# Two transformer layers on one core: the first chunk's normalization moved ahead of a weight split, loads reordered, pools with dependencies by tile, one set of maxima moved behind the second score step

## The chip, the cores and the metric

One core of a Trainium2 chip runs the whole program. The metric is the device time of one execution in microseconds (us); the time given for a kernel is the median of several executions. An execution that goes through the hardware profiler leaves a trace, and the profile is a set of views of that trace.

## The reference

`x` has 2048 rows of 448 numbers. Two layers are applied, and both use the same weights. Each layer is attention and a feed-forward part, each on a normalized copy of `x` and added to it:

```python
def _A_ref(x, wq, wk, wv, wo):          # 16 heads of 28, one k and one v for all heads
    q = (x @ wq).reshape(B, S, H, Dh).transpose(0, 2, 1, 3)
    k = x @ wk
    v = x @ wv
    scores = jnp.einsum("bhqd,bkd->bhqk", q, k) * (Dh ** -0.5)
    p = _softmax(scores, axis=-1)
    o = jnp.einsum("bhqk,bkd->bhqd", p, v)
    return o.transpose(0, 2, 1, 3).reshape(B, S, H * Dh) @ wo

def _B_ref(x, w_gate, w_up, w_down):    # 448 -> 1792 -> 448
    return (_silu(x @ w_gate) * (x @ w_up)) @ w_down

x = x + _A_ref(_layernorm(x), wq, wk, wv, wo)
x = x + _B_ref(_layernorm(x), w_gate, w_up, w_down)
# the same two lines once more, with the same weights
```

## The kernel before

**Precision.** Every float32 operand of a matmul is split into a high and a low part, and a product is high·high + high·low + low·high. So for weights there are a raw tile (`wr`, and `wq` for the other half), a high tile `wh`, made by a cast on ACT, and a low tile `wl`, raw minus high. For activations they are `xh` and `xl`.

**Order.** The instructions of each engine run in the order in which the program records them. The waits between engines are semaphores that the framework places from the accesses to tiles. For a pool opened without `reuse_waits`, the first use of a region that an earlier pool has held waits for the earlier pool as a whole; with `reuse_waits="tile"`, it waits for the tiles that have held just those bytes. DMAs go through two queues, that of SP and that of ACT, and eight semaphores are handed out to them in turn, so a DMA can also wait for the one eight places before it.

**Stages.** The 2048 rows are four chunks of 512 (`NC`). A layer has three stages.

*Projection.* Each chunk is normalized (`norm_steps`: statistics on DVE, the scale `rstd` on POOL, `xn` on DVE), transposed by PE against an identity (`flip`, L246), split into `xh` and `xl`, and multiplied with the weights of q, k and v. There are 16 units (chunk c, column group m), the groups in the order `TURN` = 3, 2, 0, 1, and each has 11 matmuls (`product_T`, L272). ACT copies the result out (L497, L498), and SP stores it to DRAM: q to `qd` (L499), k to `kt` (L502). DVE and POOL place v in `vsb` (`vt`, L505). From DRAM k comes back as `keys` (L357, split on POOL) and q as `qstack` (L134, L135).

*Attention.* `scores` runs 256 steps: 16 pairs of chunk and head group, 16 blocks of 128 keys each. A step has twelve matmuls (L567): nine into `three` (three banks of PSUM, two such tiles in turn) and three into bank 7. ACT takes the exp of both (`pt1` from bank 7 at L573, `pt` from `three` at L574), and two steps later eight matmuls (`pv`, L604) add to bank 6. Bank 7 is a single one, so the next step's part for it waits until `pt1` has been taken. The score matmuls also add a bound on each row's maximum, with its sign turned, so that the exps stay in range. `maxima(c)` computes these bounds for a chunk: four matmuls (L398) into a bank, a transpose on DVE (L400), a reduction and a split, a second transpose, and a store (L411) into `rows` of DRAM; `rows(i)` (L391) loads them into `qstack`. The maxima of chunks 0 to 2 are computed inside units 6, 10 and 14 of the projection, those of the last chunk in `finish`, behind the last unit and ahead of the first step, in bank 6:

```python
            while self.seen < len(self.order):
                self.project()
            if not full:
                self.maxima(NC - 1, (6,))
```

*Feed-forward.* `rest` runs the matmuls of `by_rows` (L292) for all groups of the 1792 columns, with ACT, DVE and POOL adding the results to `xres` (L739 to L743). The projection of the second layer is threaded into the end of the first layer's feed-forward part.

**The head.** The program starts with four loads of chunk 0 of x on SP's queue (L890, tiles of 128 rows into `xres`). PE runs `IDLE` transposes of the identity, whose result nobody reads (L898). `load_wqkv` loads the projection weights in two halves: z = 1 (half of wq, and wk) on ACT's queue, z = 0 (the other half of wq, and wv) on SP's. Each matrix comes by two DMAs (`rows3`, L130 and L131): the first 384 rows in one, and the last 64 rows, read twice into the two halves of the partitions, in the other. Behind them ACT's queue gets chunk 1 of x (L887), and SP's later gets chunks 2 and 3. `part(z)` makes `wh` and `wl` of one half, the 224 columns of q first and then the 32 of k or v (L189 on ACT, L191 on DVE for z = 1, on POOL for z = 0). Then this order is recorded:

```python
    fs, got = norm_steps(0)
    for f in fs[:5]:      # statistics and scale
        f()
    parts[0]()            # the z = 1 half: wh, wl
    for f in fs[5:]:      # xn
        f()
```

After this come the transposes of chunk 0, `parts[1]` and the units.

**A second pass.** `forward` runs once; it is run again with `full=True`, in a slower and safer form, if one of the softmax sums is out of range. With these inputs the second pass does not run.

Of the kernel before, what the change touches and what calls it, by code (L numbers as in the profile page):

```python
# [23 lines left out]
NC = S // 512  # L24
# [5 lines left out]
LEAD = 4  # L30
LIMIT = 2.0**40
TURN = (3, 2, 0, 1)
IDLE = 50


@with_exitstack
# [18 lines left out]
def forward(  # L55
# [14 lines left out]
    nc = tc.nc  # L70
# [96 lines left out]
    def load_wqkv(pool, first):  # L167


        wh = pool.tile([P, 4, 512], F32R, name="wh")  # L170
        wl = pool.tile([P, 4, 512], F32R, name="wl")

        def load(z):
            if first and not z:
                r = halves("wq2").bitcast(F32).rearrange("p a (b n) -> p (a b) n", n=256)
            else:
                r = wpool.tile([P, 4, 2, P], F32, name="wr").rearrange("p k b n -> p k (b n)")
            nc.gpsimd.memset(r[:, :, 252:256], 0.0)
            eng = nc.scalar if first and z else nc.sync
            rows3(r[:, :, 0:224], wq[:, 224 * z : 224 * z + 224], eng)  # L180
            rows3(r[:, :, 224:252], wk if z else wv, eng)
            return r

        def part(z, r):
            hi, lo = (w[:, :, 256 * z : 256 * z + 256].rearrange("p k (b n) -> p k b n", b=2) for w in (wh, wl))
            for cols, n0, n1 in ((r[:, :, 0:224], 0, 112), (r[:, :, 224:256], 112, 128)):
                raw = cols.rearrange("p k (b n) -> p k b n", b=2)
                if first:
                    nc.scalar.copy(hi[:, :, :, n0:n1], raw)  # L189
                    eng = nc.vector if z else nc.gpsimd  # L190
                    eng.tensor_tensor(lo[:, :, :, n0:n1], raw, hi[:, :, :, n0:n1], ALU.subtract)  # L191
                else:
                    split(hi[:, :, :, n0:n1], lo[:, :, :, n0:n1], raw)

        if first:
            r1, r0 = load(1), load(0)
            return [lambda: part(1, r1), lambda: part(0, r0)], (wh, wl)
        for z in (1, 0):
            part(z, load(z))
        return [], (wh, wl)  # L200
# [102 lines left out]
    class Attention:  # L303
# [86 lines left out]
            dst = qts[i % 3][28:125:32, :, :].rearrange("j z (b w) -> j (z b) w", w=32)  # L390
            nc.sync.dma_start(dst.bitcast(F32), src)  # L391

        def maxima(self, c, cands=ALL):


            pm = bank(cands)[1]
            for n, g in enumerate(TURN):
                nc.tensor.matmul(pm, kd[0:112, g, :], self.hi[g], start=(n == 0), stop=(n == 3))  # L398
            side = pers.tile([P, 512], F32, name="sg")
            nc.vector.transpose(side, pm)  # L400
            ng = pers.tile([P, 64], F32, name="ng")
            nc.vector.tensor_reduce(ng, side.rearrange("p (n k) -> p n k", k=8), AX.X, ALU.max, negate=True)
            two = pers.tile([P, 4, 2, 16], F32R, name="two")
            hi, lo = two[:, :, 0, :], two[:, :, 1, :]
            ng = ng.rearrange("p (b j) -> p j b", j=4)
            nc.vector.tensor_copy(hi, ng)
            nc.vector.tensor_tensor(lo, ng, hi, ALU.subtract)
            flat = pers.tile([P, P], F32, name="flat")
            nc.vector.transpose(flat, two.rearrange("p j z b -> p (j z b)").bitcast(F32))
            self.rowsof[c] = dram.tile([P, P], F32, name=f"rows{self.layer}_{c}")  # L410
            nc.sync.dma_start(self.rowsof[c], flat)  # L411
# [100 lines left out]
        def finish(self):  # L512

            wide.append(ALL)
            if self.layer:
                nc.scalar.activation(warm, halfn[:, 0:1], AF.Exp)
                if not full:
                    self.fetch((3, 2))
                    self.fetch((0, 1))
            while self.seen < len(self.order):  # L520
                self.project()
            if not full:
                self.maxima(NC - 1, (6,))
            for n in sorted(self.when):
                for f in self.when[n]:
                    f()
            self.advance(len(self.steps), NM + KC * LEAD)
            wide.append(LOW)

        def scores(self, ff):  # L530
            next(switch)
            with tc.tile_pool(name=f"at{self.layer}", bufs=1) as wp:
                woh = wp.tile([P, NG, D], F32R, name="woh")
                wol = wp.tile([P, NG, D], F32R, name="wol")
                on, accs, pts = {}, {}, {}
# [115 lines left out]
                for n in range(last):  # L651
                    i, kt = divmod(n, NT)
                    if kt == 4 and 2 < i + 2 < len(GR):
                        self.stack(i + 2)
                    if kt == 7 and 2 < i + 2 < len(GR):
                        self.parts(i + 2)
                    if kt == 9 and 2 < i + 2 < len(GR) and not full:
                        self.rows(i + 2)
                    if i in (2, 3) and kt == 8:
                        load_wo(i - 2)  # L660
                    if n == NT and ff.nxt:
                        ff.nxt.below(nc.sync)
                    if kt == 8 and 10 < i <= 11 + FG:
                        ff.W[i - 11] = weights(i - 11)
                    step(n)
                    if not full:
                        between_steps(n)
                    if n > 1:
                        pv(n - 2)
                    if full:  # L670
                        between_steps(n)
                    if n in due:
                        due.pop(n)()
                    if i in (5, 13, 14) and kt > 5:
                        for f in {5: fs, 13: fs1, 14: ff.second[0][:5]}[i][kt - 6 : kt - 5]:
                            f()
# [19 lines left out]
    class FeedForward:  # L696
# [157 lines left out]
            nc.vector.tensor_reduce(whole, row[0:1, 0:P], AX.X, ALU.min)  # L854

        def rest(self, xb):
            self.stage = xb.enter_context(tc.tile_pool(name=f"stage{self.layer}", bufs=2))
            self.xbp = xb.enter_context(tc.tile_pool(name=f"xb{self.layer + 1}", bufs=3))
            xd = xb.enter_context(tc.tile_pool(name=f"xd{self.layer}", bufs=1))
            self.xd = [xd.tile([P, 512], F32R, name=f"xd{c}") for c in range(NC)]  # L860
            dma(self.xd[0][64:128, :], self.X[0][0][0:64, 3, :])
            self.X[0] = (*self.X[0][:2], self.xd[0])
# [8 lines left out]
            for gi, fs in enumerate(groups):  # L871
# [6 lines left out]
                        if gi or c:  # L878
                            self.unit(gi, c, n)
                if gi == len(groups) - 2 and self.nxt:  # L880
                    self.nxt.w = load_wqkv(xb.enter_context(tc.tile_pool(name="wqkv1", bufs=1)), None)[1]
            if self.nxt:
                self.nxt.project()
            self.flush()
# [1 line left out]
    def load_x(c, eng):  # L886
        eng.dma_start(xres[:, 4 * c : 4 * c + 4, :], xs[:, 4 * c : 4 * c + 4, :])  # L887

    for t in range(4):
        nc.sync.dma_start(xres[:, t, :], xs[:, t, :])  # L890
    xb = ExitStack()
    at = Attention(0)
    at.pool = xb.enter_context(tc.tile_pool(name="stage_", bufs=3))
# [4 lines left out]
        nc.tensor.transpose(idle[:, 0:P], ident, ident)  # L898
    parts, at.w = load_wqkv(xb.enter_context(tc.tile_pool(name="wqkv0", bufs=1)), True)
    nc.gpsimd.memset(halfn, -0.5)  # L900
    load_x(1, nc.scalar)
    nc.scalar.activation(warm, halfn[:, 0:1], AF.Exp)
    nc.gpsimd.memset(bottom, 0.0)
    nc.gpsimd.memset(bottom[0:1, :], 1.0)
    fs, got = norm_steps(0)
    for f in fs[:5]:
        f()
    parts[0]()
    for f in fs[5:]:
        f()  # L910
    at.norms[0] = got
    for c in (2, 3):
        load_x(c, nc.sync)
    at.below(nc.sync)
    at.X = {c: xtile(xpool if c == 0 else xbp) for c in range(NC)}
# [18 lines left out]
    for layer in range(2):  # L934
# [6 lines left out]
        at = ff.nxt  # L941
# [28 lines left out]
```

## Time and profile before

| | us |
|---|---|
| median of 3 executions | 2043.53 |
| lowest, highest | 2042.91, 2044.38 |
| the profiled execution: span, first to last instruction | 2041.5 |
| PE busy | 2018.5 (99%) |
| ACT busy | 1311.0 (64%) |
| POOL busy | 536.7 (26%) |
| DVE busy | 460.0 (23%) |
| exps of the 512 `three` tiles (L574) | 741.2 |
| mean granted PE clock over the span, full = 1 | 0.995 |

By the trace the first layer's projection ends at about 70 us, its attention runs from 72 to 596, and the feed-forward part to 1040; the second layer's projection ends at about 1079 and its attention at 1604.

The page and the views use one form of line: engine, line of the kernel, operation, destination <- sources, partitions x elements and type, count. In the timeline a line begins with the start and the time until the end of the group, and the bracket at its end names how long the engine had been idle and what released it. `PEld` is the load of the stationary operand into PE, `SPq` and `ACTq` are the DMA issues of the two queues. In the windows the columns are the stretch, its length, the busy time of PE, PEld, DVE, ACT and POOL in it with their instruction counts, the granted clock, the share of the 16 DMA engines and GB/s. The chain of waits goes back from the last instruction, at each step to what released it.

### The profile page before, as it was taken

Reading aid. Unit: us, or ns where it says so; the run is one execution under the profiler, and the core shown is the slowest. Engines: PE = TensorE matmul, PEld = TensorE weight load, DVE = VectorE, ACT = ScalarE, POOL = GpSimd, SP = SyncE. Lnnn points to the kernel's source line nnn. Section 1 sums busy time; section 2 is a strip of 40 time slices with the busy share of each in tenths; the row PEclk is TensorE's granted clock in tenths of the full one; section 3 lists DMA queues with packets and bytes.
Section 4 is the critical chain, followed back from the end, with each engine's and each line's share of the span. In section 5 each row is a group of like instructions: output and inputs, shape, how many; then the busy total and the mean of one; then the engine's idle time right before and its main releaser. Section 6 shows DMA issues by size and latency. Waiting matters only on the chain.

```text
span 2041.5 us, 43675 instructions
## 1 busy us (share of the span) xinstructions
PE 2018.5 (99%) x18627; PEld 1275.7 (62%) x18627; DVE 460.0 (23%) x890; ACT 1311.0 (64%) x2152; POOL 536.7 (26%) x601
## 2 busy tenths in 40 slices
PE   8999999999999999999999999999999999999998
PEld 7533434334348999999883334343343689988887
DVE  6300101001104323222451001010011242232322
ACT  3699898997973333333348998979979533333332
POOL 4313121021302333333341221111222122333320
PEclk9999999999999999999999999999999999999999
DMA  4201000011100111100031110100110000111102
GB/s 146 66 22 28 21 12 22 12 37 27 32 12 19 31 31 31 31 16 26 21 93 34 30 30 12 22 12 22 27 45 13 25 17 20 31 31 31 31 1 74
DMA packets 76512, 63.44 MB, mean 31 GB/s; under 512 B 22904, under 2 KB 63224, under 8 KB 76312
## 3 DMA queue, kind: packets, MB, share of 16 engines
q1 hardware_dynamic: 74580, 58.93, 10.4%
q8 instruction: 147, 2.41, 0.5%
q10 hardware_dynamic: 1732, 1.66, 0.3%
q14 instruction: 53, 0.43, 0.1%
HBM read 47.72 MB, written 12.32 MB: 29 GB/s over the span
## 4 chain that ended last, share of the span: by engine, by line
PE 50%; ACT 46%; DVE 1%; issue 1%; DMA 1%; POOL 0%; ACTq 0%; SPq 0%; DVEq 0%; POOLq 0%
PE bank L292 39%; ACT pt L574 31%; ACT pt L573 15%; PE bank L272 4%; PE three L551 2%; PE bank L551 2%; PE bank L246 1%; PE bank L604 1%; DMA wr<-in_A_wk_dram 1%; PE three L567 0%; DVE xl L253 0%; DMA kt<-stage 0%; DVE xn L229 0%; PE bank L398 0%; DVE vt L505 0%
## 5 line engine op out<-in xcount | busy, mean ns | idle before, releaser
L574 ACT ACTIVATE pt<-three 128x1536 f32<-128x1536 f32 x512 | 741.2, 1448 | 0.0
L604 PE MATMUL bank<-pt,vsb 128*32 128x512 f32 x4096 | 547.0, 606 | 0.5 <-ACT pt L574 0.5
L567 PEld LDWEIGHTS three<-qstack,keys 32*128 32x128 f32 x4608 | 252.9, 183 | 449.7 <-ACT pt L573 393.2
L567 PE MATMUL three<-qstack,keys 32*128 32x512 f32 x4608 | 498.5, 426 | 2.3 <-DVE vt L505 1.1
L567 PE MATMUL bank<-qstack,keys 32*128 32x512 f32 x1536 | 493.5, 426 | 2.9 <-ACT pt L573 2.9
L292 PE MATMUL bank<-xh,wgh 64*128 64x512 f32 x1728 | 447.6, 390 | 0.4
L292 PE MATMUL bank<-xh,wgl 64*128 64x512 f32 x1404 | 368.2, 390 | 0.0
L573 ACT ACTIVATE pt<-bank 128x512 f32<-128x512 f32 x512 | 305.8, 597 | 74.3 <-PE bank L567 68.1
L292 PE MATMUL bank<-xl,wgh 64*128 64x512 f32 x1296 | 335.1, 390 | 0.0
L292 PE MATMUL bank<-wdh,h 64*128 64x448 f32 x1792 | 331.2, 364 | 1.2 <-ACT h L827 0.8
L292 PEld LDWEIGHTS bank<-xh,wgh 64*128 64x128 f32 x1728 | 262.9, 184 | 19.1 <-DVE xl L253 1.5
L743 POOL TENSOR_TENSOR xres<-stage,xres 128x448 f32<-128x448 f32 x108 | 127.4, 1199 | 497.9 <-ACT stage L742 497.9
L638 POOL TENSOR_TENSOR o<-o 128x512 f32<-128x512 f32 x32 | 41.1, 1285 | 821.5 <-DMA o<-rd 748.5
L292 PEld LDWEIGHTS bank<-wdh,h 64*128 64x128 f32 x1792 | 242.5, 184 | 15.2 <-issue 2.7
L567 PEld LDWEIGHTS bank<-qstack,keys 32*128 32x128 f32 x1536 | 244.3, 183 | 4.5 <-ACT pt L573 4.3
L299 ACT COPY seen<-bank 128x1 f32<-128x1 f32 x664 | 81.7, 163 | 247.3 <-PE bank L292 244.4
L292 PEld LDWEIGHTS bank<-xh,wgl 64*128 64x128 f32 x1404 | 216.6, 184 | 13.8
L292 PE MATMUL bank<-wdl,h 64*128 64x448 f32 x896 | 217.7, 366 | 0.0
L825 ACT ACTIVATE sg<-bank 128x512 f32<-128x512 f32 x112 | 67.3, 601 | 220.0 <-PE bank L292 214.9
L292 PEld LDWEIGHTS bank<-xl,wgh 64*128 64x128 f32 x1296 | 196.3, 184 | 10.5
L604 PEld LDWEIGHTS bank<-pt,vsb 128*32 128x32 f32 x4096 | 80.9, 108 | 190.0 <-issue 175.2
L826 DVE TENSOR_TENSOR sg<-bank,sg 128x512 f32<-128x512 f32 x112 | 77.4, 691 | 500.0 <-ACT sg L825 491.1
(115 smaller groups left out, 1736.6 us busy)
## 6 DMA issues: line engine op xcount, KB each, us to landing
o<-rd SPq DMA_DIRECT2D x32, 256.0 KB
qd<-stage SPq DMA_DIRECT2D x32, 224.0 KB
qraw<-qd SPq DMA_DIRECT2D x128, 56.0 KB
wdr<-in_B_w_down_dram SPq DMA_DIRECT2D x28, 224.0 KB
wr<-in_B_w_gate_dram SPq DMA_DIRECT2D x28, 192.0 KB
wr<-in_B_w_up_dram SPq DMA_DIRECT2D x28, 192.0 KB
out_dram<-xres SPq DMA_DIRECT2D x15, 224.0 KB
wrk<-kt SPq DMA_DIRECT2D x8, 256.0 KB
```

Source lines behind the costliest of these rows:

```text
L272: nc.tensor.matmul(po, a, b, start=(i == 0), stop=(i == len(seq) - 1))
L292: nc.tensor.matmul(po, a, b, start=start, stop=stop, skip_group_check=True)
L299: nc.scalar.copy(seen[:, i : i + 1], po[:, 0:1])
L551: nc.tensor.matmul(po[:, 0:D], a[:, g, ts_], b[:, g, :], start=(g + z == 0), stop=(g == NG - 1 and z == 2))
L567: nc.tensor.matmul(three[:, j, :] if j < 3 else one, k[js, kp, ks], q[js, part, :], start=(z == 0), stop=(z == 2), tile_position=(32 * j, 0),)
L573: nc.scalar.activation(pt1, one, AF.Exp, scale=SCALE)
L574: nc.scalar.activation(pt, three, AF.Exp, scale=SCALE)
L604: nc.tensor.matmul(accs[i][32 * j : 32 * j + 32, :], vsb[:, kt, :], pts[n][j], start=(kt == 0), stop=(kt == NT - 1), skip_group_check=True,)
L638: nc.gpsimd.tensor_tensor(rb, oraw, rb, ALU.mult)
L743: nc.gpsimd.tensor_tensor(r, s, r, ALU.add)
L825: nc.scalar.activation(sg, pg[0], AF.Silu)
L826: nc.vector.tensor_tensor(sg, pg[1], sg, ALU.mult)
```

## The change

- `IDLE` is 36 instead of 50.
- In `part`, POOL and DVE change places for the low parts: z = 1 on POOL, z = 0 on DVE.
- Of the four loads of chunk 0 of x, the second and fourth go to ACT's queue.
- Chunk 1 of x is loaded from SP's queue, together with chunks 2 and 3, and no longer from ACT's behind the weights.
- `xn` of chunk 0 is recorded ahead of `parts[0]`.
- The last chunk's maxima leave `finish`. They are recorded in `scores`, behind the second step, and still use bank 6.
- The pools `at`, `stage`, `xb`, `xd` of both layers and `wqkv1` of the second are opened with `reuse_waits="tile"`.

```diff
-IDLE = 50
+IDLE = 36
...
                 if first:
                     nc.scalar.copy(hi[:, :, :, n0:n1], raw)
-                    eng = nc.vector if z else nc.gpsimd
+                    eng = nc.gpsimd if z else nc.vector
                     eng.tensor_tensor(lo[:, :, :, n0:n1], raw, hi[:, :, :, n0:n1], ALU.subtract)
...
-        def maxima(self, c, cands=ALL):
+        def maxima(self, c, pm=None):
-            pm = bank(cands)[1]
+            pm = bank(ALL)[1] if pm is None else pm
...
             while self.seen < len(self.order):
                 self.project()
-            if not full:
-                self.maxima(NC - 1, (6,))
...
-            with tc.tile_pool(name=f"at{self.layer}", bufs=1) as wp:
+            with tc.tile_pool(name=f"at{self.layer}", bufs=1, reuse_waits="tile") as wp:
...
                     step(n)
                     if not full:
+                        if n == 1:
+                            self.maxima(NC - 1, banks[6])
                         between_steps(n)
...
-            self.stage = xb.enter_context(tc.tile_pool(name=f"stage{self.layer}", bufs=2))
-            self.xbp = xb.enter_context(tc.tile_pool(name=f"xb{self.layer + 1}", bufs=3))
-            xd = xb.enter_context(tc.tile_pool(name=f"xd{self.layer}", bufs=1))
+            self.stage = xb.enter_context(tc.tile_pool(name=f"stage{self.layer}", bufs=2, reuse_waits="tile"))
+            self.xbp = xb.enter_context(tc.tile_pool(name=f"xb{self.layer + 1}", bufs=3, reuse_waits="tile"))
+            xd = xb.enter_context(tc.tile_pool(name=f"xd{self.layer}", bufs=1, reuse_waits="tile"))
...
-                    self.nxt.w = load_wqkv(xb.enter_context(tc.tile_pool(name="wqkv1", bufs=1)), None)[1]
+                    self.nxt.w = load_wqkv(xb.enter_context(tc.tile_pool(name="wqkv1", bufs=1, reuse_waits="tile")), None)[1]
...
     for t in range(4):
-        nc.sync.dma_start(xres[:, t, :], xs[:, t, :])
+        (nc.scalar if t % 2 else nc.sync).dma_start(xres[:, t, :], xs[:, t, :])
...
-    load_x(1, nc.scalar)
...
     for f in fs[:5]:
         f()
-    parts[0]()
     for f in fs[5:]:
         f()
+    parts[0]()
     at.norms[0] = got
-    for c in (2, 3):
+    for c in (1, 2, 3):
         load_x(c, nc.sync)
```

## The prediction

> **What bounds the kernel now.** I read the page first: its span, the busy shares and the chain of waits that ended last.
>
> ```profile
> span 2041.5 us, 43675 instructions
> PE 2018.5 (99%) x18627; PEld 1275.7 (62%) x18627; DVE 460.0 (23%) x890; ACT 1311.0 (64%) x2152; POOL 536.7 (26%) x601
> PE 50%; ACT 46%; DVE 1%; issue 1%; DMA 1%; POOL 0%; ACTq 0%; SPq 0%; DVEq 0%; POOLq 0%
> 2.96 10.91 DMA wr<-in_A_wk_dram
> ```
>
> The chain alternates between the matmuls and the exps; the change alters neither their number nor their size. What it can move is the little that is neither: the head, where the fourth row (the chain in order of time) shows the wk load as the one long transfer, and the places where projection hands over to attention. So I read the timeline there: 0 to 24 us, 66 to 88 us (layer 0), 1074 to 1094 us (layer 1).
>
> ```profile
> 1.54 8.24 PE L898 MATMUL bank<-ident 128*128 128x128 f32 x50 [1.54 <-POOL wr L178]
> 9.18 1.03 POOL L222 TENSOR_TENSOR rstd<-rstd,halfn 128x4 f32<-128x4 f32 x1
> 9.87 0.94 ACT L189 CAST wh<-wr 128x896 fp32r<-128x896 f32 x1 [0.68 <-DMA wr<-in_A_wq_dram]
> 13.96 0.30 ACT L189 CAST wh<-wr 128x128 fp32r<-128x128 f32 x1 [3.16 <-DMA wr<-in_A_wk_dram]
> 14.56 1.78 DVE L229 TENSOR_SCALAR xn<-xres,mv,rstd 128x448 f32<-128x448 f32 x4
> 15.12 4.30 PE L246 MATMUL bank<-ident,xn 128*128 128x128 f32 x16 [5.34 <-DVE xn L229]
> 16.90 0.59 ACT L252 CAST xh<-bank 128x512 fp32r<-128x512 f32 x1 [2.64 <-PE bank L246]
> 19.07 0.78 PE L272 MATMUL bank<-xh,wh 128*128 128x512 f32 x1
> 20.07 0.59 PE L272 MATMUL bank<-xh,wl 128*128 128x512 f32 x1
> 20.50 0.40 PE L272 MATMUL bank<-xh,wh 128*128 128x512 f32 x1
> 20.73 0.39 PE L272 MATMUL bank<-xl,wh 128*128 128x512 f32 x1
> ```
>
> In the head everything queues behind wk: its cast at 13.96, a subtract on DVE that reads the cast, behind that the normalization (which needs only x and rstd), the transposes, and the first projection matmul at 19.07. The matmuls start 0.43 us apart up to 20.50 and 0.23 us apart from there.
>
> ```profile
> 69.78 1.34 PE L398 MATMUL bank<-q,kdiag 112*128 112x512 f32 x4
> 72.01 0.50 PE L567 MATMUL three<-qstack,keys 32*128 32x512 f32 x3 [0.89 <-DVE vt L505]
> 73.91 0.60 ACT L573 ACTIVATE pt<-bank 128x512 f32<-128x512 f32 x1 [2.86 <-DVE two L406]
> 74.56 0.50 PE L567 MATMUL bank<-qstack,keys 32*128 32x512 f32 x1 [1.35 <-ACT pt L573]
> 83.76 0.60 ACT L573 ACTIVATE pt<-bank 128x512 f32<-128x512 f32 x1
> 84.57 0.50 PE L567 MATMUL three<-qstack,keys 32*128 32x512 f32 x3
> 85.48 1.07 PE L604 MATMUL bank<-pt,vsb 128*32 128x512 f32 x8
> 85.65 0.60 ACT L573 ACTIVATE pt<-bank 128x512 f32<-128x512 f32 x1
> 1080.27 0.50 PE L567 MATMUL three<-qstack,keys 32*128 32x512 f32 x3 [0.67 <-DMA qstack<-rows]
> 1082.92 0.60 ACT L573 ACTIVATE pt<-bank 128x512 f32<-128x512 f32 x1 [2.42 <-DMA qd<-stage]
> 1091.81 0.60 ACT L573 ACTIVATE pt<-bank 128x512 f32<-128x512 f32 x1
> ```
>
> In both layers the first exp (73.91, 1082.92) comes late though the first step of scores began at 72.01 and 1080.27. A step takes 0.91 us of PE (84.57 to 85.48), so its scores were ready, about 0.1 us of latency added, at 73.0 and 1081.3. In layer 1 the releaser is named: the stores of q and k. In layer 0 the named DVE instruction is long done by then, and the same stores are what remains. Steady exps are 1.90 us apart (83.76 to 85.65).
>
> The third thing is the granted clock (columns of the windows: stretch, length, then busy time of PE, PEld, DVE, ACT, POOL, granted clock, DMA share, GB/s):
>
> ```profile
> 12.00:12.50 0.50, 0.00 (x0) 0.00 (x0) 0.00 (x0) 0.00 (x0) 0.00 (x0) 1.00 0.14 42
> 13.50:14.00 0.50, 0.00 (x0) 0.00 (x0) 0.00 (x0) 0.04 (x1) 0.00 (x0) 0.66 0.84 294
> 20.00:21.00 1.00, 1.00 (x5) 0.75 (x4) 0.89 (x2) 1.00 (x3) 0.03 (x1) 0.76 0.13 46
> 71.68:75.10 3.42, 1.74 (x23) 1.26 (x24) 3.27 (x5) 1.19 (x2) 2.88 (x7) 1.00 0.33 112
> 75.10:78.51 3.41, 3.29 (x21) 1.32 (x20) 0.31 (x1) 3.02 (x4) 0.00 (x0) 0.50 0.16 32
> 78.51:81.92 3.41, 3.41 (x24) 1.04 (x20) 0.00 (x0) 1.82 (x3) 0.34 (x1) 0.50 0.27 78
> 1082.03:1085.44 3.41, 1.48 (x16) 0.71 (x16) 2.72 (x5) 2.52 (x4) 2.21 (x4) 1.00 0.03 10
> 1085.44:1088.86 3.42, 3.42 (x21) 1.02 (x21) 0.00 (x0) 3.04 (x3) 0.00 (x0) 0.50 0.23 58
> ```
>
> The clock changes on a grid of 3.41 us. A stretch with 1.74 or 1.48 us of PE work is followed by half clock; one of 3.29 us did not bring it back, 3.41 and 3.42 us did. In the head it fell within 13.5 to 14.0 (mean 0.66) and came back within 20 to 21 (mean 0.76, so at about 20.48).
>
> **The change part by part.** *Head.* The normalization now stands ahead of the first weight half, so it no longer waits for wk. rstd is there at 10.2 in the old order and, with x on two queues, somewhat earlier in the new one; xn's 1.78 and the transposes' 4.30 us (at half clock) behind it end by about 14. What sets the start is then wk's cast. When wk lands follows from two rows: at 12.00 the DMA share is 0.14, two of 16 engines, and they carry 42 GB/s. These are the pieces that duplicate 64 rows; sizes from the list of DMA issues:
>
> ```profile
> xres<-in_A_x_dram SPq DMA_DIRECT2D x4, 224.0 KB
> wr<-in_A_wq_dram ACTq DMA_DIRECT2D x1, 336.0 KB
> wr<-in_A_wq_dram ACTq DMA_DIRECT2D x1, 112.0 KB
> ```
>
> Each of the two carries 1/16 of the wide loads and half of each duplicating one: x 4 x 14, twice 21 and twice 56 KB for the two halves of wq, and for wk 1/8 of that, 2.6 and 7: 220 KB up to wk's landing at 13.9. In the new order both queues are equally long ahead of wk's last piece, so wv's 9.6 KB join: at 42/2 = 21 KB per us 0.5 us, 14.4. Lower bound 14.0, about as now. Upper bound: the larger packets of the other queue win turns at the end, and wk waits for some 40 KB more, 2 us: 16.5. I take 15.0, so wk lands later than now, not earlier. From there: cast 0.30, first xh cast 0.59, 0.15 of latencies: first matmul at 16.05 against 19.07. But until 20.48 the clock is half in both orders, since in the new one PE idles from about 14 to 16, which leaves the stretch 13.65 to 17.07 as empty as those that lost the clock. By then the new order has done (20.48 - 16.05 - 0.3)/0.43 = 9.6 matmuls, the old one three. Lead: 6.6 x 0.227 = **1.5 us** (2.1 with wk at 14.0, 0.7 at 16.5). The projection has PE as its bound, so the lead lasts; I take 1.4, the middle of the bounds.
>
> Moved along at no price: the subtract on POOL (2.57 us for a half, next row) is covered by the wait for wk: from about 13.7 to 16.3, first wanted by the third matmul at 16.9. With wk at 14.0 it would cost 0.4. The idle transposes end at 1.54 + 36 x 8.24/50 = 7.5; xn comes at 9 to 10, where nothing else wants PE. The chunk-1 load moves from ACT's to SP's queue, behind wv, ahead of the loads of chunks 2 and 3. Its first reader, DVE, comes at 20.80 now and about 19.4 after; behind wk's 15.0 its 56 KB take 2.7 us, 17.7, so it lands 1.7 us ahead. The pools of the feed-forward part wait by tile: their first POOL user shows what waits there now, and it is ACT's stage, no DMA. Zero.
>
> ```profile
> 20.97 2.57 POOL L191 TENSOR_TENSOR wl<-wq,wh 128x896 fp32r<-128x896 f32 x2 [2.14 <-ACT wh L189]
> 20.80 0.63 DVE L216 BATCH_NORM_STATS2 stats<-xres 128x6 f32<-128x448 f32 x1
> 630.50 1.24 POOL L743 TENSOR_TENSOR xres<-stage,xres 128x448 f32<-128x448 f32 x1 [1.32 <-ACT stage L742]
> ```
>
> *Joints.* The first exp no longer waits for the stores: 73.91 becomes 73.1 (0.8), 1082.92 becomes 1081.4 (1.5). The maxima (four matmuls, 4 x 0.227 = 0.9 us at full clock; the row's 1.34 holds a wait for q) leave the place ahead of step 0, where they cost nothing, since step 0 waits for vt or its rows anyway. They now stand between step 1 and step 2. Queued behind them are step 2 and the first pv. At full clock there is room: bank 7 is freed 0.65 us after an exp starts (73.91 to 74.56), step 1 has 0.7 us of work left after that, so maxima run from 74.5 to 75.4 on the unshifted clock and step 2's part waits for the second exp until 75.7. The SP queue gets the row store about 3 us later relative to step 0; its reader is a later chunk's step.
>
> The clock decides the rest. Four steps at 1.90 after the first exp would be 81.5 and 1090.5; the fifth exp came at 83.76 and 1091.81, so half clock costs 2.2 and 1.3 now. With none at all the joints would give 0.8 + 2.2 = 3.0 and 1.5 + 1.3 = 2.8. I placed the new instructions on the grid with these durations, doubled at half clock. PE still idles ahead of step 0 (in layer 0, shifted by 1.4, from 68.6 to 70.6) and 0.6 us before step 1, so the clock drops one grid mark earlier: 71.68 and about 1078.6. For layer 0 that reads: first exp 71.7, bank 7 free 72.35, step 1 at half clock to 73.9, maxima to 75.5, full clock from 75.10, step 2 to 76.4, third exp 76.5, fifth 80.3 against 83.76: 3.5, of which the head's 1.4, so 2.1 for the joint. The same in layer 1 gives 1.6. If the clock needs two marks to come back, the slower step 2 and pv leave 0.5 and 0.3. The new stretch has about 0.6 us of idle PE, which by the 3.29 us row is not enough; but by that row's own gaps (a wait for an exp, one for pv) it was not much fuller, and a shift of 0.6 us in the head moves the idle out of the stretch. I take means: 0.45 x 0.5 + 0.40 x 2.1 + 0.15 x 3.0 = **1.5** for layer 0; 0.25 x 0.3 + 0.45 x 1.6 + 0.30 x 2.8 = **1.6** for layer 1.
>
> Sum: 1.4 + 1.5 + 1.6 = 4.5. The profiled execution would go from 2041.5 to 2037.0. The runs' median, 2043.53, lies 2.03 above the span; I carry that over: **2039.0 us**.
>
> **Rivals.** *No half clock at the joints.* For it: the idle times there shrink. Against it: the same grid dropped the clock after 1.74 us of work, and the idle ahead of step 0 stays. Price: 1.4 + 3.0 + 2.8 = 7.2, 2036.3. Chance 0.14. The Trainium skill (TensorE: Matmul & The Clock Gate, Part 1: The HAM clock gate) lets the clock fall after at least one idle window of about 3.4 us, free-running against the kernel; by that rule no joint would drop it, and 2036.3 would follow. The trace agrees with the window's length (75.10 to 78.51) and not with the rule: the longest PE wait ahead of 75.10 was 1.35 us.
>
> *The clock stays low for two windows at both joints*, as the 3.29 us row says: 1.4 + 0.5 + 0.3 = 2.2, 2041.3. Chance 0.16.
>
> *The first exp meets another wait in the old one's place.* Step 0's rows and vt come when they came; if the first pv or the second step waits as long as the stores did, only the head is left: 2043.53 - 1.4 = 2042.1. Against it: the rows' DMA has landed by 1080.27, 2.6 us before the stores. Chance 0.04.
>
> *Slower: wk's last piece is starved in the head.* The chunk loads now follow wv on SP's queue without waiting for it, while wk's small pieces are still in ACT's. They spread over all engines, 56 KB a chunk on each. If all three pass wk on its two engines, 168 KB take 8.0 us at 21 KB per us, or 10.6 at the 220/13.9 = 15.8 of the whole head: wk at 22.4 to 25, taken as 24, the first matmul at 25. By then the old order has done (25 - 20.5)/0.227 + 3 = 23 matmuls, and the new one starts at half clock, up to 1.7 us more: 23 x 0.227 + 1.7 = 6.9 lost, less the joints' 3.1: +3.8, 2047.3 (2045.5 to 2048.5 over wk's two ends). It decides from the point where the head loses more than 3.1 us, wk landing at about 20. For it: x's chunk 1 could share ACT's queue before and now cannot. Against it: the old order had wq's duplicating piece on SP beside wk and wk landed no later for it. Chance 0.09. The Trainium skill (DMA: Bandwidth & Descriptors, Queues, rings and completion order) says that an engine takes turns between the rings packet by packet and that a leading broadcast of c copies keeps a DMA on c engines; the 0.14 at 12.00 agrees with the second, and the first, with wk's packets the smaller, speaks against this change.
>
> **How the numbers follow.** 0.57 for the forecast, whose own range is 2037.0 to 2040.8 (head 0.7 to 2.1, joints 2.0 to 4.4); 0.14, 0.16, 0.04, 0.09 for the rivals. The range reaches to the first rival and past the third: 2036.0 to 2042.2. What a measurement of this kernel can tell from no change is about 0.2%, 4.1 us: faster means below 2039.4. Some 0.65 of the forecast's case lie below, 0.37; with the first rival 0.51, and a little for wk landing early on a shorter queue: 0.53. Slower, above 2047.6, needs the upper half of the starved wk, or that together with a missed clock mark: 0.08. The rest is 0.39.
>
> **What would show it.** Head: xn before wk's cast, that cast at 14.4 to 16.5, the first projection matmul some 1 us later, and the clock back at about 20.5. If the cast comes after 18, the starving is right. Joints: the first exp 1.0 to 1.1 us after step 0 starts, maxima between steps 1 and 2, one stretch of half clock from a mark between step 0 and step 1. The layer-0 steady exps should be 2.9 us earlier than now, those of layer 1 4.5. The forecast is wrong if the first matmul is later than 18, if half clock fills two stretches at both joints, or if the feed-forward parts change in length at all.

## The result, and the profile after

| | before | changed |
|---|---|---|
| median of 20 executions, us | 2043.67 | 2039.88 |
| lowest to highest, us | 2042.72 to 2045.51 | 2037.82 to 2042.42 |
| span of the profiled execution, us | 2041.5 | 2038.9 |
| ratio, 95% interval | | 0.9981 (0.9974 to 0.9987) |

The kernel is 3.8 us faster, 0.19%; 2039.0 was forecast. The ratio's interval lies below 1, but the gain is not clear of the 0.2% that the prediction called the least that can be told. The new kernel's executions spread over 4.6 us, the old one's over 2.8.

The page of the changed kernel, first its span, then the busy times and the chain by engine:

```profile
span 2038.9 us, 43612 instructions
PE 2015.1 (99%) x18613; PEld 1271.5 (62%) x18613; DVE 457.7 (22%) x890; ACT 1310.6 (64%) x2152; POOL 537.7 (26%) x601
PE 50%; ACT 46%; issue 1%; DMA 1%; DVE 1%; SPq 0%; ACTq 0%; POOL 0%; DVEq 0%; POOLq 0%
```

The bound is the same. The head, in the timeline of the changed kernel:

```profile
8.98 1.78 DVE L229 TENSOR_SCALAR xn<-xres,mv,rstd 128x448 f32<-128x448 f32 x4 [1.44 <-POOL rstd L222]
9.55 2.91 PE L246 MATMUL bank<-ident,xn 128*128 128x128 f32 x16 [2.08 <-DVE xn L229]
13.43 0.94 ACT L189 CAST wh<-wr 128x896 fp32r<-128x896 f32 x1 [5.61 <-DMA wr<-in_A_wq_dram]
14.45 2.50 POOL L191 TENSOR_TENSOR wl<-wr,wh 128x896 fp32r<-128x896 f32 x2 [3.39 <-ACT wh L189]
15.38 0.30 ACT L189 CAST wh<-wr 128x128 fp32r<-128x128 f32 x1 [1.01 <-DMA wr<-in_A_wk_dram]
16.21 0.79 PE L272 MATMUL bank<-xh,wh 128*128 128x512 f32 x1 [3.75 <-ACT xh L252]
20.94 0.63 PE L272 MATMUL bank<-xh,wl 128*128 128x512 f32 x1
22.49 0.40 PE L272 MATMUL bank<-xh,wh 128*128 128x512 f32 x1
```

The transposes are done at 12.5. PE then waits 3.75 us, and the weights set the start, wk last: its cast comes at 15.38, where 13.96 was before. The first matmul comes at 16.21 instead of 19.07. But the pitch of 0.23 us begins only at about 22.2 here and began at 20.50 before. Half clock is no longer than it was, two stretches of the grid, but it ends 1.8 us later (22.29, in the windows below, against 20.48), so it covers the projection's first 14 matmuls instead of three.

The joints, in the timeline of the changed kernel (L565, L571 and L602 are before's L567, L573 and L604):

```profile
71.56 0.50 PE L565 MATMUL three<-qstack,keys 32*128 32x512 f32 x3 [2.06 <-DVE vt L505]
72.57 0.60 ACT L571 ACTIVATE pt<-bank 128x512 f32<-128x512 f32 x1 [1.96 <-PE bank L565]
73.22 0.57 PE L565 MATMUL bank<-qstack,keys 32*128 32x512 f32 x1 [0.48 <-ACT pt L571]
74.58 2.07 PE L398 MATMUL bank<-q,kdiag 112*128 112x512 f32 x4
83.13 0.60 ACT L571 ACTIVATE pt<-bank 128x512 f32<-128x512 f32 x1
1080.04 0.51 PE L565 MATMUL three<-qstack,keys 32*128 32x512 f32 x3 [1.76 <-DMA qstack<-rows]
1081.06 0.60 ACT L571 ACTIVATE pt<-bank 128x512 f32<-128x512 f32 x1 [0.76 <-PE bank L565]
1082.60 1.20 PE L398 MATMUL bank<-q,kdiag 112*128 112x512 f32 x4
1088.60 0.60 ACT L571 ACTIVATE pt<-bank 128x512 f32<-128x512 f32 x1
```

Both first exps come 1.0 us after step 0, and PE, not a store, releases them. The idle time of PE ahead of step 0 has grown to 2.06 us (0.89 before), since the maxima no longer lie in it. They lie behind step 1 and took 2.07 us in layer 0, at half clock, and 1.20 in layer 1. The fifth exps (83.13, 1088.60) were at 83.76 and 1091.81.

The windows of the changed kernel on its clock grid (stretch, length, busy time of PE, PEld, DVE, ACT, POOL, granted clock, DMA share, GB/s):

```profile
12.05:15.46 3.41, 0.41 (x4) 0.17 (x2) 0.00 (x0) 1.02 (x2) 1.01 (x1) 1.00 1.07 345
15.46:18.87 3.41, 2.66 (x6) 1.83 (x7) 2.62 (x5) 3.20 (x7) 3.15 (x9) 0.50 0.96 295
18.87:22.29 3.42, 3.42 (x10) 2.65 (x9) 3.32 (x8) 0.68 (x2) 0.28 (x1) 0.50 0.23 74
70.07:73.49 3.42, 1.46 (x19) 1.05 (x23) 0.84 (x2) 1.46 (x4) 2.63 (x10) 1.00 0.58 173
73.49:76.90 3.41, 3.41 (x17) 1.83 (x17) 0.21 (x1) 2.96 (x3) 1.09 (x1) 0.50 0.07 12
76.90:80.32 3.42, 3.42 (x24) 1.01 (x24) 1.99 (x5) 1.94 (x2) 0.29 (x1) 0.50 0.25 84
1077.00:1080.42 3.42, 1.66 (x14) 1.14 (x16) 1.77 (x6) 1.17 (x2) 0.94 (x4) 1.00 0.48 144
1080.42:1083.83 3.41, 3.14 (x32) 1.64 (x24) 0.71 (x1) 2.77 (x4) 2.34 (x6) 1.00 0.24 76
```

The first row is the wait for the weights, with 0.41 us of PE work; half clock follows it. Layer 0's joint has two stretches of half clock, layer 1's none. The marks are not those of before either: 75.10 + n x 3.413 there, 73.49 + n x 3.413 here. So the lead over the old kernel is 2.9 us at the first matmul, 0.4 us at the end of layer 0's projection (its last matmul at 69.11 against 69.55), 0.6 at the fifth exp and 3.2 at layer 1's fifth.

### The profile page after: what moved, and what is told of

Same layout as the page of the kernel before. It is cut to its first block, busy times and chain, and to the rows that moved or that the text cites. A ratio compares the mean times of both kernels' runs of the same rounds, so it can differ in the third digit from the quotient of the medians.

```text
span 2038.9 us, 43612 instructions
## 1 busy us (share of the span) xinstructions
PE 2015.1 (99%) x18613; PEld 1271.5 (62%) x18613; DVE 457.7 (22%) x890; ACT 1310.6 (64%) x2152; POOL 537.7 (26%) x601
## 4 chain that ended last, share of the span: by engine, by line
PE 50%; ACT 46%; issue 1%; DMA 1%; DVE 1%; SPq 0%; ACTq 0%; POOL 0%; DVEq 0%; POOLq 0%
PE bank L292 39%; ACT pt L572 31%; ACT pt L571 15%; PE bank L272 5%; PE three L549 2%; PE bank L549 2%; PE bank L246 1%; PE bank L602 0%; PE three L565 0%; DMA wr<-in_A_wk_dram 0%; PE bank L398 0%; DMA qstack<-rows 0%; DMA xres<-in_A_x_dram 0%; DVE xl L253 0%; DVE xn L229 0%
## 5 line engine op out<-in xcount | busy, mean ns | idle before, releaser
L602 PE MATMUL bank<-pt,vsb 128*32 128x512 f32 x4096 | 546.0, 605 | 0.6 <-ACT pt L572 0.6
L565 PEld LDWEIGHTS three<-qstack,keys 32*128 32x128 f32 x4608 | 252.7, 183 | 450.6 <-ACT pt L571 393.6
L565 PE MATMUL three<-qstack,keys 32*128 32x512 f32 x4608 | 497.8, 425 | 4.1 <-DVE vt L505 2.3
L565 PE MATMUL bank<-qstack,keys 32*128 32x512 f32 x1536 | 492.6, 426 | 0.5 <-ACT pt L571 0.5
L571 ACT ACTIVATE pt<-bank 128x512 f32<-128x512 f32 x512 | 306.0, 598 | 71.6 <-PE bank L565 70.5
L565 PEld LDWEIGHTS bank<-qstack,keys 32*128 32x128 f32 x1536 | 243.9, 183 | 1.3 <-ACT pt L571 1.1
L602 PEld LDWEIGHTS bank<-pt,vsb 128*32 128x32 f32 x4096 | 80.8, 108 | 189.9 <-issue 174.2
```

Of the source, the lines that this page charges most:

```text
L565: nc.tensor.matmul(three[:, j, :] if j < 3 else one, k[js, kp, ks], q[js, part, :], start=(z == 0), stop=(z == 2), tile_position=(32 * j, 0),)
L571: nc.scalar.activation(pt1, one, AF.Exp, scale=SCALE)
L602: nc.tensor.matmul(accs[i][32 * j : 32 * j + 32, :], vsb[:, kt, :], pts[n][j], start=(kt == 0), stop=(kt == NT - 1), skip_group_check=True,)
```

## The experiments

Each was compared with runs of the kernel before on the same chip; the differences are of medians. The ratio and its interval are not worked out from the two medians, and where a run's executions fall into groups the two can differ (head filled: 6.2 us by the medians, 0.41% or 8.4 us by the ratio).

| run | median, us | before, us | difference, us | ratio, 95% interval |
|---|---|---|---|---|
| head alone | 2042.93 | 2044.05 | -1.1 | 0.9995 (0.9986 to 1.0004) |
| joints alone | 2040.06 | 2044.05 | -4.0 | 0.9982 (0.9973 to 0.9991) |
| pools alone | 2037.38 | 2044.05 | -6.7 | 0.9969 (0.9957 to 0.9981) |
| maxima alone | 2045.21 | 2044.05 | +1.2 | 1.0007 (0.9998 to 1.0017) |
| changed, maxima in front | 2037.03 | 2043.86 | -6.8 | 0.9963 (0.9950 to 0.9977) |
| changed, joints filled | 2036.63 | 2043.86 | -7.2 | 0.9963 (0.9949 to 0.9977) |
| changed, head filled | 2037.68 | 2043.86 | -6.2 | 0.9959 (0.9946 to 0.9973) |
| changed, wq in 64-row pieces | 2037.71 | 2043.86 | -6.2 | 0.9968 (0.9955 to 0.9980) |
| changed, all in 64-row pieces | 2034.26 | 2043.79 | -9.5 | 0.9953 (0.9940 to 0.9967) |
| changed, the edits costed at nothing undone | 2039.13 | 2043.79 | -4.7 | 0.9976 (0.9967 to 0.9985) |
| all that helped | 2032.08 | 2043.79 | -11.7 | 0.9941 (0.9927 to 0.9954) |

### The change in four parts

**Head alone**: on the kernel before, the hunks of the change that touch the head.

```diff
-IDLE = 50
+IDLE = 36
...
-                    eng = nc.vector if z else nc.gpsimd
+                    eng = nc.gpsimd if z else nc.vector
...
-        nc.sync.dma_start(xres[:, t, :], xs[:, t, :])
+        (nc.scalar if t % 2 else nc.sync).dma_start(xres[:, t, :], xs[:, t, :])
...
-    load_x(1, nc.scalar)
...
-    parts[0]()
     for f in fs[5:]:
         f()
+    parts[0]()
...
-    for c in (2, 3):
+    for c in (1, 2, 3):
```

> The head's part alone on the kernel before (normalization ahead, loads, 36 idle transposes, DVE and POOL exchanged); joints and pools as before. My theory: the first projection matmul comes at about 16.2 instead of 19.1, but half clock eats most of it, so the time falls by 0.7 to 2.1 us, mean 1.4 (2042.3). Rival, the lead lasts in full: -2.9. Rival, the profile's own lead of 0.5 us at 31 us is all: -0.5.

**Joints alone**: the pools and the maxima, on the kernel before.

```diff
-            if not full:
-                self.maxima(NC - 1, (6,))
...
-            with tc.tile_pool(name=f"at{self.layer}", bufs=1) as wp:
+            with tc.tile_pool(name=f"at{self.layer}", bufs=1, reuse_waits="tile") as wp:
...
+                        if n == 1:
+                            self.maxima(NC - 1, banks[6])
...
-            self.stage = xb.enter_context(tc.tile_pool(name=f"stage{self.layer}", bufs=2))
+            self.stage = xb.enter_context(tc.tile_pool(name=f"stage{self.layer}", bufs=2, reuse_waits="tile"))
...
```

> The joints' part alone on the kernel before (all pools by tile, last maxima behind step 1); the head as before. My theory: -3.1 us (2.0 to 4.4, by how many marks of the clock grid fall badly), and the first exps 1.0 to 1.1 us after step 0 begins. Rival, that the head carries the gain: -1 or less.

**Pools alone**: the same without the hunks of `maxima`.

```diff
-            with tc.tile_pool(name=f"at{self.layer}", bufs=1) as wp:
+            with tc.tile_pool(name=f"at{self.layer}", bufs=1, reuse_waits="tile") as wp:
...
```

> Only the pools by tile; the last maxima stay ahead of step 0. My theory: the first exps lose their wait for the stores just as with both (0.8 and 1.5 us earlier), step 0 still begins when its rows and vt are there, and the maxima at the old place fill an idle stretch of PE, so at least two thirds of the joints' gain is here: -2 to -3.5. Rival, that the maxima in front hold step 0: the first exp comes no more than 0.3 us earlier and the time falls by less than 1.

**Maxima alone**: the same without the pools.

```diff
-            if not full:
-                self.maxima(NC - 1, (6,))
...
+                        if n == 1:
+                            self.maxima(NC - 1, banks[6])
```

> Only the last maxima behind step 1; the pools stay as before, so the first exps still wait for the stores. My theory: no gain, the maxima only leave an idle stretch for a busier one: 0 to +1 us. Rival, the maxima held step 0: -1 to -2 and step 0 0.9 us earlier.

The head alone gives 1.1 us, and its interval holds no change. In its profile the first matmul came at 16.21 too, with only one stretch at half clock, and the projection's last matmul was 1.4 us ahead of before's. The joints give 4.0. But the pools alone give 6.7, and the maxima alone lose 1.2, with an interval that again holds no change. The gain is the pools', and with them in place the move of the maxima costs 2040.06 - 2037.38 = 2.7 us; the slowest execution with the pools alone (2038.91) lies below the fastest with both (2039.16). The timeline of the run with the pools alone shows layer 0's joint, its windows the clock there:

```profile
70.18 1.33 PE L398 MATMUL bank<-q,kdiag 112*128 112x512 f32 x4
72.12 0.50 PE L567 MATMUL three<-qstack,keys 32*128 32x512 f32 x3 [0.61 <-DMA qstack<-rows]
73.14 0.60 ACT L573 ACTIVATE pt<-bank 128x512 f32<-128x512 f32 x1 [1.69 <-PE bank L567]
74.96 0.60 ACT L573 ACTIVATE pt<-bank 128x512 f32<-128x512 f32 x1
```

```profile
69.18:72.59 3.41, 2.80 (x18) 1.86 (x20) 2.71 (x7) 1.07 (x2) 1.14 (x5) 1.00 0.53 162
72.59:76.00 3.41, 2.56 (x34) 1.30 (x28) 3.11 (x5) 2.86 (x4) 2.56 (x5) 1.00 0.17 58
76.00:79.42 3.42, 3.42 (x41) 0.97 (x33) 0.00 (x0) 3.42 (x5) 0.00 (x0) 1.00 0.15 48
```

The first exp loses its wait for the stores without the maxima's move, and step 0 starts when the rows have landed, 0.61 us after the matmuls of the maxima. PE is busy 2.80 and 2.56 us of the two stretches, where the changed kernel had 1.46, and the clock stays full.

The run with the joints shows in one trace what the move costs with and without the clock. Its layer 0 kept full clock, its layer 1 did not:

```profile
1074.29:1077.70 3.41, 1.60 (x16) 0.82 (x14) 1.81 (x4) 1.17 (x2) 0.93 (x4) 1.00 0.47 139
1077.70:1081.11 3.41, 3.18 (x19) 2.00 (x16) 0.18 (x1) 2.88 (x4) 2.77 (x6) 0.50 0.22 67
1081.11:1084.53 3.42, 3.42 (x23) 1.35 (x21) 2.21 (x5) 1.75 (x3) 0.00 (x0) 0.50 0.17 48
```

From the start of step 0 to the fifth exp it took 8.56 us in layer 0 and 11.21 in layer 1; with the pools alone it was 8.37 and 8.38. So at full clock the move costs 0.2 us a layer, and with two stretches of half clock 2.8.

### Is it the clock?

**Changed, maxima in front**: the maxima go back ahead of step 0.

```diff
             while self.seen < len(self.order):
                 self.project()
+            if not full:
+                self.maxima(NC - 1, banks[6])
...
-                        if n == 1:
-                            self.maxima(NC - 1, banks[6])
```

> The changed kernel with the last maxima put back ahead of step 0; head and pools as changed. Theory from the runs so far: the maxima at the old place fill an idle stretch and keep the clock, at the new place they cost about 2.7 us; so this is the pools' 6.4 and the head's 1.1 together, about -7.5 (2036.5), faster than the changed kernel by 3 to 4. Rival, that the parts share one gain: no faster than the pools alone, -6.4, or only as fast as the changed kernel, -3.8.

**Changed, joints filled**: the maxima stay behind step 1, and PE gets work that nobody needs in the gaps.

```diff
                     i, kt = divmod(n, NT)
+                    if n < 2 and not full:
+                        for _ in range((9, 3)[n]):
+                            nc.tensor.transpose(banks[6][:, 0:P], ident, ident)
```

> The changed kernel with transposes of the identity, whose result nobody reads, on PE at the joints: nine ahead of step 0, three between steps 0 and 1. No stored value depends on them. If idle PE and the half clock after it are what the moved maxima cost, this gives 2 to 3.5 us over the changed kernel (-6 to -7) and no half clock at the joints. If the maxima cost because they stand in a busy stretch, it gives 0.5 or less (-4).

Both are faster than the changed kernel by 3 us or more by their medians. The second settles it: twelve instructions more in each layer, the maxima where the change put them, and 3.4 us less (7.2 against 3.8). The intervals of the two ratios overlap by 0.0003, but all five of its executions lie below the lowest of the changed kernel's 20. Its windows:

```profile
66.79:70.20 3.41, 3.41 (x21) 2.87 (x20) 2.88 (x6) 1.03 (x3) 0.00 (x0) 1.00 0.29 88
70.20:73.62 3.42, 2.24 (x26) 1.39 (x27) 0.77 (x2) 1.35 (x3) 2.69 (x10) 1.00 0.59 175
73.62:77.03 3.41, 3.41 (x33) 1.57 (x29) 1.45 (x3) 3.41 (x5) 1.02 (x1) 1.00 0.08 10
```

In place of 1.46 us stand 2.24, and the clock stays full in both layers. From step 0 to the fifth exp it takes 8.56 and 8.57 us. So the moved maxima cost by the idle time they leave at the joint and the half clock after it, and hardly by the place they take. How the filling should be shared out, nine ahead of step 0 and three ahead of step 1, was not tried. With the maxima in front the expected 7.5 was nearly met (6.8), but the head's part of it does not show beside the pools' 6.7.

**Changed, head filled**: the same for the wait for the weights.

```diff
     at.turned(0)
+    for n in range(20):
+        nc.tensor.transpose(banks[3][:, 0:P], ident, ident)
```

> The changed kernel with 20 more such transposes behind those of chunk 0, where PE waits for the weights. Theory: half clock at the start of the projection is what eats the head's lead, so the first projection matmul stays at about 16.2 and the projection begins at full clock: 1.5 to 3 us over the changed kernel (-5.3 to -6.8). Rival, the projection's first units are set by DVE and by chunk 1's arrival: 0 to 0.5.

In its profile wk's cast came at 15.96 and the first matmul at 16.80, later than in the changed kernel's, but at full clock: the last matmul of layer 0's projection is at 67.33 instead of 69.11. That is 1.8 us, and the medians differ by 2.4 (6.2 against 3.8). The five executions fall into two groups, two at about 2033.5 and three at 2037.7; the profiled one is of the slower group and has two stretches of half clock at layer 0's joint.

### What holds the weights?

**Changed, wq in 64-row pieces**: two DMAs of 64 partitions in place of one that reads the rows twice, for wq.

```diff
-        eng.dma_start(dst[:, 3], src[384:448, :][None].to_broadcast([2, 64, n]))
+        if n < 100 or not two:
+            eng.dma_start(dst[:, 3], src[384:448, :][None].to_broadcast([2, 64, n]))
+        else:
+            for b in range(2):
+                eng.dma_start(dst[64 * b : 64 * b + 64, 3], src[384:448, :])
...
```

> The changed kernel with the last 64 rows of wq loaded by two DMAs of 64 partitions each instead of one that reads them twice. If the duplicating pieces on two engines are what makes the weights late, the casts come at 7 to 10 instead of 13.4 and 15.4, the first projection matmul at 12 to 13.5, and 1.5 to 3 us are won over the changed kernel (less where half clock eats it). Rival, wk waits for something else, the issue of its DMAs or the queue's order: the cast stays at 14 to 15 and the time within 0.5.

**Changed, all in 64-row pieces**: the same for wk and wv too, without the condition on `n`.

> The changed kernel with every duplicating piece of the head (wq, wk, wv) loaded by two DMAs of 64 partitions each. In the run before, where only wq's were split, wq came early and wk's cast stayed at 14.95: theory, its many small packets on two engines take turns with the chunk loads of x. Then here wk's cast comes at 9 to 11 and the first projection matmul, behind the transposes, at 12 to 13: 1 to 3 us over the changed kernel (-5 to -7). Rival, the order of the queues or the issue holds wk: cast at 14 or later, first matmul at 15 to 16, time as the changed kernel within 1.

The timelines, first with wq alone, then with all:

```profile
8.14 1.09 ACTq L132 DMA_DIRECT2D wr<-in_A_wk_dram  x1
8.69 1.47 SPq L891 DMA_DIRECT2D xres<-in_A_x_dram  x3
10.67 0.93 ACT L193 CAST wh<-wr 128x896 fp32r<-128x896 f32 x1
14.95 0.30 ACT L193 CAST wh<-wr 128x128 fp32r<-128x128 f32 x1 [3.35 <-DMA wr<-in_A_wk_dram]
15.78 0.79 PE L276 MATMUL bank<-xh,wh 128*128 128x512 f32 x1 [3.37 <-ACT xh L256]
```

```profile
8.11 1.12 ACTq L133 DMA_DIRECT2D wr<-in_A_wk_dram  x2
9.14 1.49 SPq L891 DMA_DIRECT2D xres<-in_A_x_dram  x3
10.66 1.12 ACT L193 CAST wh<-wr 128x896 fp32r<-128x896 f32 x2
12.61 0.78 PE L276 MATMUL bank<-xh,wh 128*128 128x512 f32 x1
14.25 0.73 PE L276 MATMUL bank<-xh,wl 128*128 128x512 f32 x1 [0.41 <-POOL wl L195]
```

With wq alone split, wq's cast moves from 13.43 to 10.67, and wk's stays: its last piece, issued from 8.14, is there only at 14.95, though all of this half's wq is there by 10.67; three chunks of x are issued beside it from 8.69. With wk and wv split as well, the issue is as late (8.11), the same chunks follow (from 9.14), and both casts are done at 11.8. So it is the narrow form, the load that duplicates its rows, that holds wk.

What it takes turns with, the DMA packets of the traces show. With wq alone split, the packets between 9.5 and 14.5 us are 129 on ACT's queue (0.01 MB, wk's piece) and 864 on SP's (1.52 MB), of which only 16 are under 512 bytes. A narrow piece of wk or wv has 112-byte rows, so wv's was through by then, and wk's ran beside the chunk loads. In the changed kernel itself it was wv's piece: from 12.1 to 14.4 us ACT's queue moved 178 packets under 512 bytes and SP's 189.

With all in pieces the first matmul comes at 12.61, right behind the transposes, and the third waits 0.41 us for POOL's subtract: the next bound. The time of the run with wq alone is inconclusive: its executions spread from 2034.0 to 2042.5, and the profiled one, the slowest, has two stretches of half clock at each joint. With all split they lie within 1.7 us.

**Changed, the edits costed at nothing undone**:

```diff
-IDLE = 36
+IDLE = 50
...
-                    eng = nc.gpsimd if z else nc.vector
+                    eng = nc.vector if z else nc.gpsimd
...
-            self.stage = xb.enter_context(tc.tile_pool(name=f"stage{self.layer}", bufs=2, reuse_waits="tile"))
+            self.stage = xb.enter_context(tc.tile_pool(name=f"stage{self.layer}", bufs=2))
...
```

(`xb`, `xd` and `wqkv1` likewise; `at` keeps its waits by tile.)

> The changed kernel with the edits that I costed at nothing taken back: 50 idle transposes, DVE and POOL as before, the pools of the feed-forward part and of the second weights without waits by tile. Theory: all of them lie behind other work, so the time stays within 0.7 us of the changed kernel (-3.8). Rival, one of them carries part of the gain: at least 1.5 slower than the changed kernel.

4.7 us under before, against 3.8 with these edits: by the medians 0.9 better, a little over the 0.7 expected, and the two intervals overlap. They carry none of the gain. The move of chunk 1's load, costed at nothing as well, was not undone here.

**All that helped**:

```diff
-IDLE = 36
+IDLE = 48
...
-                    self.at(13, lambda i=i: self.rows(i))
+                    self.at(9 + 2 * i, lambda i=i: self.rows(i))
...
+            if not full:
+                for _ in range(6):
+                    nc.tensor.transpose(banks[6][:, 0:P], ident, ident)
+                self.maxima(NC - 1, banks[6])
...
+                    if n == 1 and not full:
+                        for _ in range(3):
+                            nc.tensor.transpose(banks[6][:, 0:P], ident, ident)
...
-                        if n == 1:
-                            self.maxima(NC - 1, banks[6])
```

With the pieces of 64 rows for all weights of the head.

> All that helped, together, on the changed kernel: the maxima ahead of step 0, six idle transposes ahead of them and three ahead of step 1, the loads as in the run with every piece split, 48 idle transposes in the head, and the first steps' rows loaded after units 9, 11 and 13 instead of all after 13. Theory: joints 6.4 and head 3 to 5, so -9.5 to -11.5 (2032.5 to 2034.5), with no half clock but at the end. Rival, the gains overlap since all of them buy clock: -7 to -8.

2032.08 us, 11.7 under before and 7.9 more than the change won; 9.5 to 11.5 were expected. The gains over the changed kernel, 3.4 with the joints filled and 5.7 with all in pieces, add nearly in full, and the profile has half clock in one stretch of the head and at the end only. What the earlier loads of the rows (`self.rows`) and the transposes ahead of maxima in front are worth was not tried alone.

## Why the prediction was right, and where not

- **The sum.** 4.5 us were forecast, 3.8 measured. The terms were 1.4 for the head and 3.1 for the joints; alone they measure 1.1, with an interval that holds no change, and 4.0. The two together won less than their sum of 5.1; the intervals of the runs (1.2 to 1.8 us to each side) are too wide to say that this is more than their spread. The joints' 3.1 was a mean over ways in which the clock's marks can fall, 1.5 for layer 0 and 1.6 for layer 1. In the profiled execution the time from step 0 to the fifth exp fell from 11.75 to 11.57 us in layer 0 and from 11.54 to 8.56 in layer 1: 0.2 and 3.0. Neither layer went as forecast, and that the two add up to the forecast is luck in that one execution. The steady exps, said to come 2.9 and 4.5 us earlier, came 0.6 and 3.2 earlier (the fifth).
- **Head.** wk's cast at 15.0 and the first matmul at 16.05 were forecast, 15.38 and 16.21 came. That half clock would eat most of the lead was right, and the run with the head filled shows it: it starts 0.6 us later and yet is 1.8 us earlier at the end of the projection. wk's narrow piece did move beside wv's, as the sum had it (the packets of 12.1 to 14.4 us above). The transposes, put at half clock with 4.30 us, took 2.91 at full clock; nothing hung on it, since the weights came later. The end of half clock, set at 20.48 as before, was not to be had from one execution: it came at 22.3, and at 20.4 in the run of the head alone.
- **The store waits.** Right: the first exps follow step 0 by 1.0 us, as forecast, and the pools are what did it.
- **The maxima.** Here the working failed. It said that ahead of step 0 "they cost nothing", and behind step 1 at full clock nothing either; it found the idle time ahead of step 0 and the clock that drops from it, but took that idle time as given. The maxima were what filled it. The pools alone were never worked out; they would have shown that the move loses 2.7 us of the 6.7. The total still came out near, since the clock's loss was in the joints' terms: the right sum for a change whose two parts pull against each other, which the prediction did not see.
- **The clock's return.** By the 3.29 us row, a stretch with no PE idle in the records should bring it back. 73.49 to 76.90 had 3.41 us and did not, while in the head of the run with all in 64-row pieces 11.36 to 14.77, at half clock, had 3.00 us of work and did. Layer 0 took two stretches and layer 1 none, so neither rule held; in the total the mean over the outcomes (4.5) came nearer to the 3.8 than two stretches (2.2) or one (1.4 + 2.1 + 1.6 = 5.1) at both joints would have.
- **The edits at nothing** carried no gain, as forecast. The stretch between the joints, from layer 0's last exp to the last projection matmul of layer 1, was 485.0 us before and 485.1 after (593.00 to 1078.04, 592.82 to 1077.89), so it did not change either.
- **The rivals.** No half clock at all came true in layer 1 only; the pools alone had none at either joint, and their profile came close to that rival's price for the joints, 3.0 and 2.8: from step 0 to the fifth exp they were 3.4 and 3.2 us shorter than before. The starved wk did not occur in the changed kernel (15.38), but the run with wq alone in 64-row pieces shows wk's narrow piece beside the chunk loads, as that rival had it, with its cast at 14.95 though wq's came at 10.67. That an idle stretch of about 3.4 us is needed to lower the clock, the rule of the Trainium skill (TensorE: Matmul & The Clock Gate, Part 1: The HAM clock gate), is again not what the traces show: 2.06 us of waiting, 1.46 us of work in the stretch, and half clock from 73.49. That the window runs free against the kernel they do show: the marks of the two executions differ by 1.8 us (22.29 against 20.48).

## What to carry to other kernels

Work of an engine whose clock follows its load is not free to move out of an idle stretch: ask what the stretch is without it, and whether useless work there is cheaper than the clock. A change with two parts at one place should be priced part by part, or a good part hides a bad one. A load that duplicates its rows with a leading broadcast ran on two of the 16 DMA engines here (a share of 0.14 at 12.00 in the old kernel); splitting such loads into plain ones of 64 partitions took the changed kernel from 3.8 to 9.5 us under before, where the new order of the head alone gave 1.1.

## What was not expected of the hardware

Busy time in the records does not decide the clock alone. At the joints half clock mostly followed stretches of 1.20 to 1.74 us of PE work (1.20 in the run with wq alone in pieces), but layer 1 of the changed kernel kept full clock after 1.66, and so did the maxima alone after 1.72 (from 68.25) and the run with the edits at nothing undone after 1.74 (from 1076.34). With the maxima in front, one joint lost it after 2.78, as the windows of that run show:

```profile
1076.39:1079.80 3.41, 2.78 (x28) 1.38 (x24) 3.27 (x5) 3.26 (x4) 2.77 (x6) 1.00 0.22 67
1079.80:1083.22 3.42, 3.42 (x21) 1.04 (x20) 0.31 (x1) 2.34 (x3) 0.00 (x0) 0.50 0.14 47
```

What else counts, the runs leave open. The spread of the changed kernel's executions goes along with the clock: the slowest, 2042.42 us, was granted 0.994 of full clock in the mean, the fastest, 2037.82, 0.997.
